# A fixed order for the Strassen products of a 256-token stage, with the next unit's first product ahead of the odd unit's seventh

## The chip, the cores and the metric

One Trainium2 chip, one of its cores. The metric is the device time of one execution in microseconds (us), lower is better; a kernel's figure is the median of several runs. Each core has five engines that work side by side and wait for one another through semaphores: TensorE (matrix products; PE in the profile, PEld for its weight loads), VectorE (DVE), ScalarE (ACT), GpSimd (POOL) and SyncE (SP). Each engine runs its own instructions strictly in the order in which the program lists them.

## The reference

Attention over 8 batches of 12 heads (448 tokens, head size 64), and its output, reshaped to 3584 tokens of 768 values, through a gated feed-forward block:

```python
def _attn_ref(q, k, v):
    scale = 1.0 / np.sqrt(q.shape[-1])
    scores = scale * np.matmul(q, k.transpose(0, 1, 3, 2))
    scores = scores - np.max(scores, axis=-1, keepdims=True)
    attn = np.exp(scores)
    attn = attn / (np.sum(attn, axis=-1, keepdims=True) + 1e-09)
    return np.matmul(attn, v).astype(np.float32)

def _moe_ref(x, w_gate, w_val, w_out):
    g = x @ w_gate                          # 3584x768 by 768x1536
    silu = g * (1.0 / (1.0 + np.exp(-g)))
    val = x @ w_val
    return (silu * val @ w_out).astype(np.float32)
```

## The kernel before

The kernel works in float16 with float32 sums. Attention goes over pairs of heads; the feed-forward block for tokens that are ready is woven between attention steps, so that TensorE always has something to do. When attention is over, two stages are left in which the first half of the feed-forward block (gate and value products) is computed with Strassen's method in its seven-product form: one of 256 tokens by 256 tokens (the subject here), and one later of 448 by 448. Between them and at the end come groups of output products (`out_group`, L694).

**A unit.** The class `Unit` covers two of the 12 blocks of 128 feature rows, for gate (even unit number u) or value (odd u), and two halves of tokens. There are 12 units, 0 to 11. The 768 input values are split in two halves, so each unit is a 2x2 by 2x2 block product, and its four result blocks need seven products P1 to P7 instead of eight. A product (L817) is three matmuls of 128x128 weights by 128x256 tokens, into one of three PSUM areas: `a` and `e`, the two banks of a tile `un` (three such tiles in rotation), and `b`, a tile `ub` (two in rotation). The steps of one unit, and what each waits for:

- P1 starts `a`. A1 (ScalarE, L859) copies `a` to `b`. P2 then adds to `a`, whose sum is result block 00.
- P5 starts `e`. A2 (ScalarE, L863) copies `e` to SBUF, into a buffer `kept` (p5).
- P6 adds to `b`, after A1. D1 (VectorE, L866) writes `b` + p5 into `e`, after P6 and A2. P3 then adds to `e`: result block 01.
- P7 adds to `b`, after D1, which has to read `b` first. D2 (VectorE, L870) writes `b` + p5 into a second `kept` buffer in SBUF: result block 11.
- P4 adds to `b`, after D2, which has to read `b` first: result block 10.
- F00, F01, F10 and F11 read the four result blocks out. Of a gate unit ScalarE does it (L882: silu into SBUF); of a value unit VectorE does it (L884: silu times value, to `hts`). The two value blocks in `un` and the one in `ub` are in PSUM; block 11 lies in SBUF as `kept`, so F11 of an odd unit reads both of its inputs, silu and `kept`, from SBUF.

So five of the seven products wait for nothing but P1's or P5's place or for copies made early, while P6 waits for A1, P7 for D1 and P4 for D2: between these, products of the neighbouring unit are put in.

**What sets the order.** `unit_items` makes a dictionary of items: name (such as `P6_4`, product P6 of unit 4), engine, a duration taken for it, the names that it comes after, and the function that emits it. `order_of` plans the items of all engines with these durations, and with a latency from engine to engine (0.22 us behind TensorE, 0.07 behind VectorE and ScalarE): again and again it takes the item that could start first, or one on the same engine within 0.12 us of it that stands earlier in the dictionary. The instructions are emitted in the order of the planned starts, and each engine then runs its own in that order. Nothing is planned anew on the chip.

**Beside the units.** GpSimd makes the sums of weights that P3, P5, P6 and P7 take as stationary operand (`weight_sums`, L780 to L783: four sums of 128x384 elements of float16, items `W_6` to `W_11`), well ahead of the units that need them, and after them half of the sums for the first output group (L555 to L558, items `G0` to `G7`). All of these read and write SBUF. Item `O` is one output product group (L665) that stands ahead of the last P4.

Of the kernel before, what the change touches and what calls it, by code (L numbers as in the profile page):

```python
# [65 lines left out]
def kernel(  # L66
# [17 lines left out]
    NFB = DF // 128  # L84
# [358 lines left out]
    def pv_open(pr, one=False):  # L443
        if one:
            acc = ps_s.tile([128, 2, 512], FP32, tag="s", name="acc")
            accs[pr] = [acc[:, hx] for hx in range(2)]
        else:
            accs[pr] = [ps_f.tile([128, 512], FP32, tag="f", name="acc") for _ in range(2)]
# [457 lines left out]
    with tc.manual_schedule():  # L906
# [424 lines left out]
        def unit_items(units, make, w):  # L1331

            items = {}
            t_pe, t_act, t_dve = NK * (w / 2400 + 0.0025), 0.2 + w / 1280, 0.2 + w / 1050

            def begin(u):
                units[u] = make(u)
                units[u].P1()

            for u in range(NFB):  # L1340
                old_s = [f"{k}_{u - 3}" for k in ("F00", "F01")] if u > 2 else []
                old_f = [f"{k}_{u - 2}" for k in ("F10", "D2")] if u > 1 else []
                items[f"P1_{u}"] = (PE_, t_pe, old_s, lambda u=u: begin(u))

                def do(name, eng, us, after, u=u):
                    items[f"{name}_{u}"] = (eng, us, after, lambda: getattr(units[u], name)())

                if u < 2:
                    do("Z", PE_, t_pe / NK, old_f)
                    old_f = [f"Z_{u}"]  # L1350
                do("A1", ACT_, t_act, [f"P1_{u}"] + old_f)
                do("P5", PE_, t_pe, [f"P1_{u}", f"W_{u}"])
                do("A2", ACT_, t_act, [f"P5_{u}"] + ([f"D2_{u - 2}"] if u > 1 else []))
                do("P6", PE_, t_pe, [f"A1_{u}"])
                do("D1", DVE_, t_dve, [f"P6_{u}", f"A2_{u}"])
                do("P7", PE_, t_pe, [f"D1_{u}"])
                do("D2", DVE_, t_dve, [f"P7_{u}"] + ([f"F11_{u - 2}"] if u > 1 else []))
                do("P3", PE_, t_pe, [f"D1_{u}"])
                do("P4", PE_, t_pe, [f"D2_{u}"])
                do("P2", PE_, t_pe, [f"A1_{u}"])  # L1360
                for f, bb, last in ((0, 0, "P2"), (1, 1, "D2"), (1, 0, "P4"), (0, 1, "P3")):
                    name = f"F{f}{bb}"
                    items[f"{name}_{u}"] = (
                        DVE_ if u % 2 else ACT_,
                        t_dve if u % 2 else t_act,
                        [f"{last}_{u}"] + ([f"{name}_{u - 1}"] if u else []),
                        lambda u=u, f=f, bb=bb: units[u].out(f, bb),
                    )
            return items
# [5 lines left out]

        units = {}
        items = unit_items(units, lambda u: Unit(u, 256, x5, t5, hts5), 256)
        p0 = NPAIR - 1
        pv_open(p0, True)
        pv_rest(p0)  # L1380
# [38 lines left out]
        items = unit_items(units, lambda u: Unit(u, S, x7, t7, hts), S)  # L1419
# [14 lines left out]
        for m, fn in enumerate(final[0][0][1]):  # L1434
            u = NFB - 1 if m else NH - 1
# [35 lines left out]
```

## Time and profile before

| | us |
|---|---|
| time before, median of 3 runs | 428.84 |
| lowest and highest of them | 428.45, 429.25 |
| the profiled execution's own time | 429.01 |
| its span (first to last instruction) | 427.2 |
| TensorE busy in it | 419.4 |
| the stage of 256 tokens, first product to first output group | 299.90 to 329.31 |
| in 299.9 to 329.3: VectorE, ScalarE, GpSimd busy | 21.04, 16.81, 28.93 |

The times of single instructions are from the profiled execution, counted from its span's start. A row of the timeline has the start in us, the duration in us, engine, line of the kernel, operation, what is written and read (`ub<-vraw,wg` writes the tile `ub` and reads `vraw` and `wg`; names are those of the buffer's first use, so sums of weights and tokens appear as `E`, `vraw`, `qkraw`, `wsum` or `vo`), sizes, the count of instructions merged into the row, and in brackets the engine's idle time before the row and what ended it. A product's row of three matmuls has a duration of 0.49 us, while the next product can start 0.33 us after it: matmuls overlap, so stalls of TensorE are seen in the distance of starts, not in the gaps. VectorE's and ScalarE's rows overlap a little for the same reason. The granted TensorE clock is 1.00 throughout this stage.

### The profile page before, as it was taken

To read this page: it belongs to the slowest core of one execution; us is meant where nothing else is said; L and a number is where in the kernel's file an instruction comes from. 1 tells how busy PE (TensorE), PEld (TensorE's weight loads), DVE (VectorE), ACT (ScalarE), POOL (GpSimd) and SP (SyncE) were. 2 spreads that over 40 slices of the span, in tenths; PEclk is the share of its full clock that TensorE was granted. 3 is DMA by queue.
4 is the path that set the end of the run, shared out by engine and by line. 5 is a ranking of instruction groups with operands and counts; after the bars stand their busy time and mean duration, and the time that the engine had idled before them with its cause. 6 is when DMAs were issued, how large, how long until landed. Compare 5 with 4: busy or idle time off the path is not lost.

```text
span 427.2 us, 11656 instructions
## 1 busy us (share of the span) xinstructions
PE 419.4 (98%) x4652; PEld 290.4 (68%) x4652; DVE 269.7 (63%) x644; ACT 245.1 (57%) x395; POOL 229.8 (54%) x351
## 2 busy tenths in 40 slices
PE   8999999999999999999999999999999999999996
PEld 3666666655457777757666677777889985555795
DVE  4766562776568665575635776677777765565663
ACT  6975667646656655646666546559655235545221
POOL 8656525989885683657654774945999000000000
PEclk9999999999999999999999999999999999999999
DMA  9999999999999699999999997923100241000125
GB/s 138 177 200 200 200 177 187 140 153 213 173 136 127 97 193 106 163 122 114 123 153 127 141 155 91 153 47 97 23 1 21 94 107 44 0 2 1 38 76 149
DMA packets 107927, 49.77 MB, mean 116 GB/s; under 512 B 59872, under 2 KB 104672, under 8 KB 107872
## 3 DMA queue, kind: packets, MB, share of 16 engines
q0 software_dynamic: 46800, 24.56, 51.5%
q1 hardware_dynamic: 60752, 24.22, 32.4%
q8 instruction: 36, 0.59, 0.6%
q10 hardware_dynamic: 320, 0.25, 0.2%
q14 instruction: 19, 0.16, 0.1%
HBM read 49.55 MB, written 11.01 MB: 142 GB/s over the span
## 4 chain that ended last, share of the span: by engine, by line
PE 92%; ACT 3%; DVE 3%; issue 1%; DMA 0%; ACTq 0%; DVEq 0%
PE gp L572 17%; PE og L694 17%; PE vp L572 12%; PE un L817 10%; PE acc L435 8%; PE ub L817 8%; PE s L344 5%; PE op L665 5%; PE acc L400 2%; PE s L374 2%; PE s L356 1%; ACT E L382 1%; PE tp L317 1%; PE op L1023 1%; PE wp L164 1%; DVE t L625 1%
## 5 line engine op out<-in xcount | busy, mean ns | idle before, releaser
L364 ACT ACTIVATE E<-s 128x896 f16<-128x896 f32 x126 | 106.6, 918 | 40.2 <-PE s L344 28.2
L572 PE MATMUL gp<-X,wg 128*128 128x384 f16 (+1 forms) x360 | 73.9, 347 | 0.0
L238 POOL COPY qk<-qkraw 128x512 f16<-128x512 f16 x70 | 42.9, 655 | 55.1 <-DMA qkT<-qk 54.6
L572 PE MATMUL vp<-X,wv 128*128 128x384 f16 (+3 forms) x360 | 66.7, 321 | 0.1
L625 DVE SCALAR_TENSOR_TENSOR t<-sg,gp 128x384 f32<-128x384 f32 (+1 forms) x60 | 36.3, 607 | 42.3 <-ACT sg L599 42.0
L572 PEld LDWEIGHTS <-wv 128*128 128x128 f16 x462 | 43.7, 98 | 25.8 <-issue 0.3
L572 PEld LDWEIGHTS <-wg 128*128 128x128 f16 x360 | 32.8, 98 | 26.3 <-issue 2.1
L178 POOL DMA_DIRECT2D vraw<-in_v_dram x72 | 44.0, 634 | 12.2 <-DMA wo<-in_moe_w_out_dram 8.2
L599 ACT ACTIVATE sg<-gp 128x384 f32<-128x384 f32 (+1 forms) x60 | 32.1, 537 | 28.6 <-PE gp L572 27.9
L382 ACT ACTIVATE E<-s 112x896 f16<-112x896 f32 x48 | 40.6, 917 | 8.7 <-PE s L374 8.7
L178 POOL DMA_DIRECT2D qkraw<-in_k_dram x70 | 42.4, 622 | 5.0 <-DMA wo<-in_moe_w_out_dram 3.6
L435 PEld LDWEIGHTS <-E 128*128 128x128 f16 (+1 forms) x1152 | 37.5, 96 | 10.8 <-issue 4.7
L694 PEld LDWEIGHTS <-hts 128*128 128x128 f16 x528 | 44.1, 98 | 0.3
L435 PE MATMUL acc<-vo,E 128*128 128x65 f16 (+1 forms) x1152 | 42.2, 192 | 0.8 <-DVE hts L631 0.6
L631 DVE SCALAR_TENSOR_TENSOR hts<-t,vp 128x384 f16<-128x384 f32 (+3 forms) x60 | 32.5, 541 | 5.9 <-PE vp L572 1.9
L465 DVE TENSOR_TENSOR xt<-acc,R 128x256 f16<-128x256 f32 x72 | 30.6, 425 | 2.5
L719 ACT ACTIVATE osb<-og 128x384 f32<-128x384 f32 x21 | 10.3, 491 | 38.0 <-PE og L694 38.0
L201 POOL DMA_DIRECT2D qkraw<-in_q_dram x43 | 29.3, 682 | 5.0 <-DMA vraw<-in_v_dram 2.2
L344 PE MATMUL s<-qkT 64*128 64x448 f16 x216 | 30.2, 354 | 0.2
L694 PE MATMUL og<-wo,hts 128*128 128x192 f16 x264 | 29.0, 246 | 0.0
L694 PEld LDWEIGHTS <-hsum 128*128 128x128 f16 x300 | 25.5, 98 | 1.0
L464 DVE RECIPROCAL R<-acc 128x4 f32<-128x4 f32 x72 | 12.7, 177 | 18.0 <-PE acc L435 17.9
(184 smaller groups left out, 713.2 us busy)
## 6 DMA issues: line engine op xcount, KB each, us to landing
vraw<-in_v_dram POOLq DMA_DIRECT2D x72, 64.0 KB, 4.7
qkraw<-in_q_dram POOLq DMA_DIRECT2D x39, 112.0 KB, 4.5
qkraw<-in_k_dram POOLq DMA_DIRECT2D x68, 64.0 KB, 4.5
wg<-in_moe_w_gate_dram POOLq DMA_DIRECT2D x8, 288.0 KB, 10.1
wv<-in_moe_w_val_dram POOLq DMA_DIRECT2D x8, 288.0 KB, 10.6
wo<-in_moe_w_out_dram POOLq DMA_DIRECT2D x2, 1152.0 KB, 18.3
out_dram<-osb SPq DMA_DIRECT2D x7, 288.0 KB, 3.7
out_dram<-osb SPq DMA_DIRECT2D x6, 336.0 KB, 3.2
```

Source lines behind the costliest of these rows:

```text
L178: eng.dma_start(dst[ts(s, 64)], rows)
L238: nc.gpsimd.tensor_copy(dst.rearrange("p c h d -> p h c d"), src)
L344: nc.tensor.matmul(s[:, hx, 0:S], lhsT=t[ts(hx, 64), ts(c + low(pr, hx), 128)], rhs=t[ts(hx, 64), ds(NC * 128, S)], start=True, stop=True,)
L364: nc.scalar.activation(e[:, 0 : 2 * S].rearrange("p (h q) -> p h q", h=2), s[:, :, 0:S], AF.Exp, scale=sm_scale)
L382: nc.scalar.activation(e[:, :, 0:S], s[0:P, :, 0:S], AF.Exp, scale=sm_scale)
L435: nc.tensor.matmul(acc[:, ts(j, D + 1)], lhsT=e[rows, ds(hx * S + j * 128, 128)], rhs=Vts[pr % NV][rows, hx, col, 0 : D + 1], start=first, ...
L572: nc.tensor.matmul(dst[:, 0:w], lhsT=wslice(kind, self.fb, cb), rhs=X[kk][:, cb, ds(c0 + lo, w)], start=(cb == 0), stop=(cb == NCB - 1),)
L599: self.readers = [nc.scalar.activation(self.sg[:, 0:n], gp[:, 0:n], AF.Tanh, scale=0.5)]
L625: nc.vector.scalar_tensor_tensor(self.t1[:, 0:n], self.sg[:, 0:n], 1.0, self.gp[:, 0:n], ALU.add, ALU.mult)
L631: nc.vector.scalar_tensor_tensor(self.hts[:, self.fb, ds(lo, w)], self.t1[:, ds(lo, w)], 0.5 * HS, vp[:, 0:w], ALU.mult, ALU.mult)
L694: nc.tensor.matmul(dst, lhsT=lhs(n), rhs=rhs(n), start=first and n == 0, stop=n == NH - 1, skip_group_check=True)
L817: mm = nc.tensor.matmul(dst, lhsT=lhs[:, n], rhs=rhs[:, n], start=first and n == 0, stop=n == NK - 1, skip_group_check=True,)
```

## The change

Behind the making of the items, a list of product names is written out, and each name in it is made to wait for the one ahead of it. The planner and everything behind it stay as they are, and so do the stage of 448 tokens and units 0 and 1 up to their last products.

```diff
         units = {}
         items = unit_items(units, lambda u: Unit(u, 256, x5, t5, hts5), 256)
+        names = ["P1_2", "P5_2"]
+        for u in range(2, NFB, 2):
+            names += f"P6_{u} P4_{u - 1} P2_{u} P1_{u + 1} P5_{u + 1} P7_{u} P3_{u} P6_{u + 1} P4_{u}".split()
+            names += f"P2_{u + 1} P1_{u + 2} P7_{u + 1} P3_{u + 1} P5_{u + 2}".split()
+        names = [name for name in names if name in items]
+        for one, two in zip(names, names[1:]):
+            items[two][2].append(one)
```

`NFB` is 12. The line of names makes, for each even u from 2 to 10, one chain over the products of units u and u+1, beginning with P6 of u and ending with P5 of u+2; names of units that don't exist are dropped, so behind P3 of unit 11 the chain ends.

## The prediction

> **What bounds the kernel now.** I read the page from the top: the busy shares, then the chain that ended last.
>
> ```profile
> span 427.2 us, 11656 instructions
> PE 419.4 (98%) x4652; PEld 290.4 (68%) x4652; DVE 269.7 (63%) x644; ACT 245.1 (57%) x395; POOL 229.8 (54%) x351
> ...
> PE 92%; ACT 3%; DVE 3%; issue 1%; DMA 0%; ACTq 0%; DVEq 0%
> ```
>
> TensorE is busy for 98% of the span and holds 92% of the chain. Only TensorE's own stalls can be removed, and every new stall of TensorE moves the end. The changed stage runs from 299.90 us (the first product of unit 0) to 329.31 us (the first output group), 29.4 us long. I then read TensorE's timeline there; one row is one product of three matmuls. The first four rows are the first and fifth product of unit 2, the fourth of unit 1 and the sixth of unit 2; the last three are the fourth product of unit 2 and the second and seventh of unit 3.
>
> ```profile
> 304.47 0.49 PE L817 MATMUL un<-X,wg 128*128 128x256 f16 x3
> 304.80 0.49 PE L817 MATMUL un<-vraw,qkraw 128*128 128x256 f16 x3
> 305.13 0.49 PE L817 MATMUL ub<-vraw,wv 128*128 128x256 f16 x3
> 305.48 0.49 PE L817 MATMUL ub<-vraw,qkraw 128*128 128x256 f16 x3
> ...
> 307.79 0.49 PE L817 MATMUL ub<-vraw,wg 128*128 128x256 f16 x3
> 308.12 0.49 PE L817 MATMUL un<-X,wv 128*128 128x256 f16 x3
> 308.52 0.49 PE L817 MATMUL ub<-vraw,wsum 128*128 128x256 f16 x3
> ```
>
> Starts lie 0.327 us apart when nothing waits (304.47 to 304.80; 14 products without a stall would take 4.58 us). The pair of units from 307.79 to 312.50 takes 4.70 us, so it stalls for 0.12 us. The rows show where: the seventh product of an odd unit starts 0.40 after the second instead of 0.327 (net 0.078 each time), and the two steps between products of the two `ub` banks take 0.35 (net 0.022 each). The profile shows no other idle time of TensorE here, so this is **all that any order can win**: over the stage's five pairs after the first, about 0.6 us, or 0.14% of the run.
>
> **The order that results.** By the planner's rule and its listed durations, TensorE's order before is P1 P5 P4' P6 P2 (even unit u, prime for u-1), then P1 P5 (u+1), P7 P3 (u), P6 (u+1), P4 (u), P2 P7 P3 (u+1). The change makes two edits per pair from unit 2 on. P6 of u goes ahead of P4 of u-1. P1 of u+2 goes ahead of P7 of u+1, so four times: units 4, 6, 8, 10. VectorE keeps its order (F10 of u-1, then D1 of u), except that D1 of unit 2 goes ahead of F10 of unit 1. ScalarE and GpSimd keep theirs. No instruction is added or removed, and no DMA moves.
>
> **Edit one, P1 of u+2 ahead of P7 of u+1.** P7 of an odd unit waits for D1, which ends 0.05 us before it. With one product more between P6 and P7 there are four, 4 x 0.327 = 1.31 us; the chain from P6 through D1 took 308.52 - 307.44 = 1.08. So these four stalls go: 4 x 0.078 = 0.31 saved. P6 of u+2 now stands four products behind its P1 instead of three, so the wait for copy A1 goes too, for units 4 to 10: 4 x 0.022 = 0.09 saved. The early P1 needs the `un` bank of u-1, whose last reader ended 3.2 us earlier (306.02 against 309.18 for unit 4): nothing lost. The stall before P4 of u is untouched (P7, P3, P6, P4 still in a row). Unit 11 has no successor, so the stall of its P7 stays. Saved together: 0.40.
>
> **Edit two, P6 of u ahead of P4 of u-1.** P6 waits for copy A1 of its unit.
>
> ```profile
> 305.06 0.37 ACT L859 ACTIVATE ub<-un 128x256 f32<-128x256 f32 x1 [1.03 <-PE un L817]
> ```
>
> For unit 2, P1 isn't moved (nothing stands ahead of it in the list). A1 ends at 305.43 and P6 can start at 305.48 at the earliest, exactly where it is. P4 of unit 1 filled that time and now comes after it: **0.33 lost**, once. For units 4 to 10 the moved P1 gives the cover back.
>
> **What is late next: VectorE.** P7 of an odd unit is now one product nearer to P7 of the next even one: eight products (2.62 us) instead of nine. Between them lies a chain on VectorE.
>
> ```profile
> 309.05 0.42 DVE L870 TENSOR_TENSOR kept<-ub,kept 128x256 f32<-128x256 f32 x1
> 309.58 0.77 DVE L884 SCALAR_TENSOR_TENSOR hts<-silu,kept 128x256 f16<-128x256 f32 x1
> 310.27 0.41 DVE L884 SCALAR_TENSOR_TENSOR hts<-silu,un 128x256 f16<-128x256 f32 x1
> 310.60 0.41 DVE L884 SCALAR_TENSOR_TENSOR hts<-silu,ub 128x256 f16<-128x256 f32 x1
> 310.93 0.42 DVE L866 TENSOR_TENSOR un<-ub,kept 128x256 f32<-128x256 f32 x1
> ```
>
> These are D2, F11, F01, F10 of unit 3 and D1 of unit 4, without a gap between the last four. D2 starts 0.53 after P7 starts (308.52), F11 0.53 after D2; from the end of F11 to P7 of unit 4 it is -0.08 (the next starts that much before the end) + 0.33 + 0.33 + 0.42 + 0.05 (VectorE's end to TensorE's start, as at 308.52) = 1.05. (F10 also waits for P4 of u-1, which edit two makes a product later; it would let F10 of unit 3 start at 310.94, earlier than the chain does below, so it holds up neither F10 nor the D1 queued behind it.) So P7 of u can start no sooner than P7 of u-1 + 1.06 + F11 + 1.05. With F11 at 0.43 that is 2.54, inside the 2.62. With the 0.77 of this row it is 2.88: a stall. Before, nine products (2.95 and 0.02) covered it, with 0.14 to spare for unit 4. So **F11 decides**, and it is the one whose time varies.
>
> ```profile
> L884 DVE SCALAR_TENSOR_TENSOR hts<-silu,kept x6: 426/680/814, 304.9 to 328.4; 128x256 f16<-128x256 f32 x6
> L884 DVE SCALAR_TENSOR_TENSOR hts<-silu,kept x6: 625/626/626, 358.2 to 397.9; 128x448 f16<-128x448 f32 x6
> ```
>
> Its six in this stage take 426 to 814 ns; the same line with 448 tokens, later, when the page shows POOL at 0, always 625 or 626. GpSimd's rows give the reason:
>
> ```profile
> 309.15 0.91 POOL L781 TENSOR_TENSOR E<-E,wg 128x384 f16<-128x384 f16 x1
> 310.02 1.09 POOL L782 TENSOR_TENSOR E<-wg,wg 128x384 f16<-128x384 f16 x1
> 311.08 0.91 POOL L783 TENSOR_TENSOR E<-wg,E 128x384 f16<-128x384 f16 x1
> ```
>
> F11 of unit 3 ends at 310.34, 0.28 after the GpSimd sum that ran when it came (310.06), and the next sum takes 1.09 instead of 0.91. The same holds for all six: the end is 0.28 after a sum's end. F11 (both inputs in SBUF) and a sum hold each other up. The Trainium skill, SBUF — State Buffer, section "Who interferes with whom", says that a VectorE instruction with two SBUF inputs and a GpSimd instruction that reads SBUF exclude each other for a whole instruction, the first one winning; the trace agrees, with these 0.28 and 1.09. Were the port shared evenly instead, each F11 would take the 0.66 that is the mean of the six, and units 4 to 10 would each stall for 1.06 + 0.66 + 1.05 - 2.62 = 0.15: +0.53 in all, in four small stalls and not in one large.
>
> **The sum.** P6 of unit 2 at 305.48, then eleven products and one 0.02: P7 of unit 3 at 309.10 (before 308.52), F11 at 310.16. The sum of L781 ends at 310.06 as before, and L782 has run since 310.02, undisturbed now: it ends at 310.93. F11 ends at 311.21 and P7 of unit 4 starts at 312.26; its turn was 309.10 + 2.62 = 311.72. **Stall 0.55.** From there six products and 0.02 to P7 of unit 5 (314.25), F11 at 315.31, GpSimd's L783 (from 314.67, 0.91) ends at 315.58, F11 at 315.86, P7 of unit 6 at 316.91 where its turn was 316.87: 0.04. The same reckoning gives 0.04 for units 8 and 10, because GpSimd's sums come round every 4.65 us, like a pair. P7 of unit 11: 327.95 instead of 327.34. In parts: +0.33 +0.55 +0.12 -0.40 = **+0.60**. The row bounds of F11's hold are 0 (it slips in at 310.06) and 0.72 (a whole sum of 0.87 plus the 0.28, less 0.43); I take 0.63, because it comes 0.14 after the start of L782, and all six rows waited for the sum that had begun. Behind the stage TensorE's output groups follow without gaps (329.31, 329.81, 330.30), so 0.60 reaches the end. The profiled execution took 429.01 (span 427.2 and 1.8 around it): 429.6 against that, and **429.4** against the median of 428.84, which lies 0.17 below it.
>
> **Rivals.**
> *F11 of unit 3 slips in* (0.2): it comes 0.10 after the sum's end at 310.06; should the hand-over be later or the phase of the sums differ by that much, F11 takes 0.43, unit 4's turn is missed by 0.02 only, and so on. +0.33 - 0.40 + 4 x 0.03 = +0.05: 428.9. Against it: the next sum is listed as started at 310.02.
> *A second miss, the slower side* (0.1): F11 of unit 5 comes at 315.31, 0.26 ahead of a sum's end. If GpSimd runs that much earlier against TensorE, it meets the following sum, and P7 of unit 6 pays some 0.55 more: +1.15, 430.0. It decides from a shift of 0.25. For it: both chains feed back on each other. Against: the lock holds them in step once they have met.
> *The order pays as written* (0.07): VectorE never holds P7, and A1 of unit 2 comes early enough: -0.40, 428.4. Against it: A1 ends 0.05 before P6 in the rows.
> The remaining 0.05 is for waits that no row shows. That the order isn't taken up can't be: each name is made to wait for the one ahead.
>
> **The numbers.** The forecast has 0.58: 429.4, itself between 429.1 and 429.8. The range 428.6 to 430.1 takes in the slip-in and most of the second miss. A measurement of this kernel tells some 0.2%, 0.86 us, from no change. Faster by that (below 427.98) is out of reach of the 0.6 that the stage stalls for: 0.03. Slower (above 429.70): the second miss and the upper edge of the forecast, 0.22. Same: 0.75.
>
> **What will show it.** P6 of unit 2 should start 0.68 after P5 of unit 2, and its P4 of unit 1 behind it. P7 of units 3, 5, 7, 9 should start 0.327 after the product before. F11 of unit 3 should take about 1.05, and P7 of unit 4 start 0.88 after P5 of unit 5; those of units 6, 8, 10 some 0.37. The forecast is wrong if F11 of unit 3 takes under 0.6, or if TensorE stalls beyond unit 4 by over 0.1.

## The result and the profile after

The changed kernel takes 430.0 us (median of 12 runs, 429.26 to 431.52) against 428.79 us for the kernel before in the same comparison. The ratio is 1.0031 with a 95% interval of 1.0024 to 1.0039: slower by 1.2 us by the medians, twice the forecast 0.60, and with the whole interval above the 0.2% that the forecast lay within. The page of the profiled execution (430.36 us), its span, its busy shares and the chain that ended last:

```profile
span 428.6 us, 11651 instructions
...
PE 419.6 (98%) x4652; PEld 290.2 (68%) x4652; DVE 270.1 (63%) x644; ACT 245.4 (57%) x395; POOL 229.5 (54%) x351
...
PE 90%; DVE 4%; ACT 3%; DMA 1%; issue 1%; ACTq 0%; DVEq 0%; SPq 0%
```

TensorE does the same work; its share of the chain falls from 92 to 90% and VectorE's rises from 3 to 4%. From the first product of unit 0 to the start of the last P4 the stage took 29.09 us before (299.90 to 328.98) and takes 30.45 now (299.88 to 330.32): 1.36 more, and the span is 1.4 longer. The piece of the chain behind it, 252 matmuls of the output groups, takes 20.79 us in both, so the whole difference arises in this stage and reaches the end.

TensorE's timeline shows where. Rows as in the prediction; the brackets at the end, which no row of before had in this stage, give TensorE's idle time and what ended it. In order: P5 and P6 of unit 2, P4 of unit 1; P5 of unit 5 and P7 of unit 4; P5 of unit 11 and P7 of unit 10.

```profile
304.78 0.49 PE L817 MATMUL un<-vraw,qkraw 128*128 128x256 f16 x3
305.46 0.49 PE L817 MATMUL ub<-vraw,qkraw 128*128 128x256 f16 x3 [0.19 <-ACT ub L859]
305.78 0.49 PE L817 MATMUL ub<-vraw,wv 128*128 128x256 f16 x3
...
311.37 0.49 PE L817 MATMUL un<-vraw 128*128 128x256 f16 x3
312.25 0.49 PE L817 MATMUL ub<-vraw,E 128*128 128x256 f16 x3 [0.38 <-DVE un L866]
...
325.94 0.49 PE L817 MATMUL un<-vraw,vo 128*128 128x256 f16 x3
326.94 0.49 PE L817 MATMUL ub<-vraw,wsum 128*128 128x256 f16 x3 [0.52 <-DVE un L866]
```

A step beyond 0.327 is a stall. The table lists those that differ, in us beyond 0.327, from the starts of the products:

| stall before | kernel before | forecast | changed kernel |
|---|---|---|---|
| P6 of unit 2 | 0.02 | 0.35 | 0.35 |
| P6 of units 4, 6, 8, 10 | 0.02 each | 0 | 0 |
| P7 of units 3, 5, 7, 9 | 0.08 each | 0 | 0 |
| P7 of unit 4 | 0 | 0.55 | 0.55 |
| P7 of units 6 and 8 | 0 | 0.04 each | 0.11 each |
| P7 of unit 10 | 0 | 0.04 | 0.68 |

Everything up to P7 of unit 4 came as worked out. The rest is 0.11 instead of 0.04 at units 6 and 8, and a second hold of F11 at unit 10. VectorE's rows for F11 of units 3 and 9:

```profile
310.13 1.05 DVE L884 SCALAR_TENSOR_TENSOR hts<-silu,kept 128x256 f16<-128x256 f32 x1
...
324.70 1.19 DVE L884 SCALAR_TENSOR_TENSOR hts<-silu,kept 128x256 f16<-128x256 f32 x1
```

and GpSimd's around the first, then two sums of the pair between (taken up further below), and those around the second, where a row with x2 holds two sums, each but a held one 0.91 long:

```profile
310.00 0.91 POOL L782 TENSOR_TENSOR E<-wg,wg 128x384 f16<-128x384 f16 x1
310.87 1.09 POOL L783 TENSOR_TENSOR E<-wg,E 128x384 f16<-128x384 f16 x1
...
319.30 0.91 POOL L780 TENSOR_TENSOR vo<-wv 128x384 f16<-128x384 f16 x1
320.29 0.97 POOL L781 TENSOR_TENSOR vo<-vo,wv 128x384 f16<-128x384 f16 x1
...
322.96 1.78 POOL L555 TENSOR_TENSOR hsum<-hts 128x384 f16<-128x384 f16 x2
324.70 1.96 POOL L556 TENSOR_TENSOR hts<-hts 128x384 f16<-128x384 f16 x2
```

F11 of unit 3 comes at 310.13, after the sum of L782 has begun, waits for that whole sum (to 310.91) and ends 0.28 later. F11 of unit 9 comes at 324.70, 0.04 ahead of the end of the sum that runs then (324.74); that is too late, the next sum, the first of L556, goes first (to 325.61), and F11 ends 0.28 after it.

### The profile page after: what moved, and what is told of

Read it like the earlier page. It is cut to its first block, busy times and chain, and to the rows that moved or that the text cites. A ratio compares the mean times of both kernels' runs of the same rounds, so it can differ in the third digit from the quotient of the medians.

```text
span 428.6 us, 11651 instructions
## 1 busy us (share of the span) xinstructions
PE 419.6 (98%) x4652; PEld 290.2 (68%) x4652; DVE 270.1 (63%) x644; ACT 245.4 (57%) x395; POOL 229.5 (54%) x351
## 4 chain that ended last, share of the span: by engine, by line
PE 90%; DVE 4%; ACT 3%; DMA 1%; issue 1%; ACTq 0%; DVEq 0%; SPq 0%
PE gp L572 17%; PE og L694 17%; PE vp L572 12%; PE un L817 9%; PE acc L435 8%; PE ub L817 8%; PE s L344 5%; PE op L665 5%; PE acc L400 2%; PE s L374 2%; PE s L356 1%; ACT E L382 1%; PE tp L317 1%; PE op L1023 1%; DVE t L625 1%; DVE hts L631 1%
```

## Experiments

The theory after the result: edit one saves 0.40; edit two costs 0.33 at unit 2; and with eight products between the seventh ones a hold of F11 by a whole GpSimd sum reaches TensorE, twice in this execution (0.55 and 0.68), beside 0.11 at units 6 and 8, where F10 waits for P4 and D1 stands behind it. Rivals: that the order itself makes the loss (the shorter distance, whatever F11 takes), or that only one of the edits does.

The effects are near what timing can tell, so each run is read in two ways: its ratio to the kernel before in the same comparison (whose median was 428.64 to 428.79), and the length of the stage in its profiled execution, from the first product of unit 0 to the start of the last P4, which shows single stalls but is one execution.

| run | median us | ratio to before, 95% interval | stage, us | against 29.09 |
|---|---|---|---|---|
| changed kernel | 430.0 | 1.0031 (1.0024 to 1.0039) | 30.45 | +1.36 |
| changed kernel, once more | 429.95 | one run | 30.44 | +1.35 |
| edit one alone | 428.71 | 0.9999 (0.9989 to 1.0009) | 28.83 | -0.26 |
| edit two alone | 430.35 | 1.0040 (1.0028 to 1.0053) | 30.73 | +1.64 |
| F11 from PSUM | 429.1 | 1.0020 (1.0009 to 1.0032) | 29.43 | +0.35 |
| GpSimd later | 429.02 | 1.0006 (0.9991 to 1.0021) | 29.43 | +0.35 |
| before, F11 from PSUM | 429.07 | 1.0002 (0.9990 to 1.0014) | 29.21 | +0.12 |
| D1 ahead of F10 | 428.81 | 0.9999 (0.9988 to 1.0010) | 29.43 | +0.34 |
| P4 of unit 1 first | 428.88 | 0.9993 (0.9975 to 1.0012) | 29.10 | +0.02 |
| all mends | 428.43 | 0.9987 (0.9975 to 0.9999) | 28.51 | -0.58 |

**Edit one alone.**

```diff
-            names += f"P6_{u} P4_{u - 1} P2_{u} P1_{u + 1} P5_{u + 1} P7_{u} P3_{u} P6_{u + 1} P4_{u}".split()
+            names += f"P4_{u - 1} P6_{u} P2_{u} P1_{u + 1} P5_{u + 1} P7_{u} P3_{u} P6_{u + 1} P4_{u}".split()
```

> Only edit one: the next unit's P1 ahead of the odd unit's P7, with P4 left ahead of P6. Theory (the head stall of unit 2, and F11 held by a GpSimd sum in the shortened VectorE chain, make the loss): no stall at P6 of unit 2; F11 of unit 3 comes at 309.83 and meets the sum that ends near 310.06, so it ends at 310.34 as before the change, and P7 of unit 4 has its turn at 311.42; every later F11 gets in 0.3 to 0.6 us before a sum's end in the same way. P7 of unit 11 at 327.1, 0.25 us ahead of before: about 428.5. Rival (the shorter distance between the seventh products costs by itself): P7 of units 4 to 10 late as in the changed kernel, at least 0.5 us slower than before.

The stage is 0.26 shorter, the 0.25 of the theory, with no stall above 0.03 between P7 of unit 1 and P7 of unit 11. (The 0.02 at P6 of units 4 to 10 is gone, but P4 of the odd unit, now three products behind P7 and not four, waits for D2 by as much.) F11 of units 3 to 9 takes 0.50 to 0.55. The distance between seventh products is the eight of the changed kernel, so that distance alone costs nothing: the rival falls. In the times the gain can't be told from zero (interval 0.9989 to 1.0009).

**Edit two alone.**

```diff
-            names += f"P2_{u + 1} P1_{u + 2} P7_{u + 1} P3_{u + 1} P5_{u + 2}".split()
+            names += f"P2_{u + 1} P7_{u + 1} P3_{u + 1} P1_{u + 2} P5_{u + 2}".split()
```

> Only edit two: P6 ahead of P4, with P1 left behind P7 and P3. Theory: A1 is too late for P6 in each of units 2, 4, 6, 8 and 10, so each P6 starts 0.68 us after P5 instead of 0.33 and nothing fills it: 5 x 0.33 = 1.65 us, 430.4. The distance from P7 of an odd unit to P7 of the next is nine products and that stall, so F11 costs nothing. Rival (edit one makes the loss, edit two is worth little): within 0.4 us of before.

TensorE's timeline has such a row for each of the five pairs (the fifth bracket names GpSimd, but there too A1 ends 0.05 ahead, at 325.61 against 325.66); the first two:

```profile
305.53 0.49 PE L817 MATMUL ub<-vraw,qkraw 128*128 128x256 f16 x3 [0.19 <-ACT ub L859]
310.56 0.49 PE L817 MATMUL ub<-vraw,E 128*128 128x256 f16 x3 [0.19 <-ACT ub L859]
```

Five steps of 0.68 instead of 0.35, the stage 1.64 longer, 430.35 us. Edit two needs edit one, in every pair. F11 of units 5 and 9 was held to 0.90 and 0.89 here and cost nothing: with nine products and a stall of A1 between the seventh ones there is room for it.

**F11 from PSUM.** Once F00 has read bank `a` out, D2 of an odd unit can put block 11 there instead of into SBUF; F11 then has one input in each memory.

```diff
     def D2(self):
+        if self.u % 2 and self.w == 256:
+            self.c22 = self.a
+            self.note(DVE_, nc.vector.tensor_tensor(self.a, self.b, self.p5, ALU.add), "a")
+            return
...
```

Two more lines, left out here, make D2 of an odd unit wait for F00 and enter F11 among the readers of that bank.

> The changed kernel, with block 11 of the odd units written to the PSUM bank a that F00 has read out, so that F11 has one input in SBUF and one in PSUM. Theory: F11 takes about 0.42 us in all six units, whatever GpSimd runs, and the sums take 0.91; the stalls of 0.55 and 0.68 at P7 of units 4 and 10 fall to the 0.11 that units 6 and 8 show (F10 waits for P4, and D1 behind it). +0.33 - 0.40 + 4 x 0.11 = +0.35 against before: 429.1. Rival (the order stalls P7 through VectorE's queue whatever F11 takes): the time of the changed kernel, 430.0.

VectorE's group of all readouts of `un` (F00, F01 and now F11, 18 in all; minimum, median and maximum in ns):

```profile
L889 DVE SCALAR_TENSOR_TENSOR hts<-silu,un x18: 414/422/422, 303.5 to 329.1; 128x256 f16<-128x256 f32 x18
```

None is held, though GpSimd runs as before, and its sums take 0.91 beside them. The stalls at P7 of units 4, 6, 8 and 10 are 0.11 each: of the 0.55 and 0.68 the holds made 0.44 and 0.57, and F10's wait of 0.11 is left. The stage is 0.35 longer than before, as worked out. In the times alone this isn't clear: the interval overlaps that of the changed kernel, and 0.35 us (a ratio of 1.0008) lies just below it.

**GpSimd later.** One more instruction on GpSimd, on an idle tile, ahead of the weight sums of unit 6.

```diff
+        items["N"] = (POOL_, 0.4, [], lambda: nc.gpsimd.tensor_add(warm[:], warm[:], warm[:]))
+        items["W_6"][2].append("N")
```

> The changed kernel with one more GpSimd instruction (128x128, a sum of an unused tile with itself) ahead of the weight sums of unit 6: GpSimd's later sums all come some 0.3 to 0.4 us later, nothing else is touched. Theory (only the phase of the sums decides): F11 of unit 3 now comes ahead of the end of the sum of L781 and gets in behind it, 0.28 us after its end, so P7 of unit 4 stalls by about 0.1 and not 0.55; the added work makes the kernel 0.4 us faster or more if unit 9 gets in too: 429.1 to 429.6. Rival (the sums only fill GpSimd's time): no change from 430.0.

The added instruction took 0.40 us. Ahead of P7 of unit 4, VectorE's F11 of unit 3 and GpSimd's sums around it:

```profile
309.83 0.54 DVE L884 SCALAR_TENSOR_TENSOR hts<-silu,kept 128x256 f16<-128x256 f32 x1
```

```profile
309.17 0.91 POOL L781 TENSOR_TENSOR E<-E,wg 128x384 f16<-128x384 f16 x1
310.05 1.09 POOL L782 TENSOR_TENSOR E<-wg,wg 128x384 f16<-128x384 f16 x1
```

Counted from the stage's first product (299.57 here, 299.88 in the changed kernel), F11 comes at 10.26 against 10.25, and L781's sum begins at 9.60 against 9.25. So F11 now comes 0.25 ahead of the end of L781's sum (310.08) instead of 0.09 behind it, gets in there and takes 0.54, not 1.05; it is L782's sum that gives way (1.09). All four stalls are 0.11, also that of unit 10. **More work made the kernel faster**, by 1.0 us of stage and from a ratio of 1.0031 to 1.0006. The phase of GpSimd's sums (how they lie in time against TensorE's products) decides over both holds: the order is the changed kernel's, and both are gone.

**The control: the kernel before with F11 from PSUM** (the same edit on the order before).

> The control: the kernel before with block 11 of the odd units in the PSUM bank a, as in the run that did this to the changed kernel. Theory (F11 costs only where eight products stand between the seventh ones, not nine): F11 falls to 0.42 in all six units as well, and nothing else moves, 0.0 us, the stage from the first product to the last P4 29.09 us as before. Rival (F11 in PSUM is faster in itself, whatever the order): some 0.5 to 1 us faster than before.

F11 fell to 0.42 here too and no stall went: the long F11 of before was covered. The stage is 0.12 longer, all of it one new stall at P7 of unit 10, where D1 waited for a product of `un`, 0.28 us after VectorE was free. Why only there isn't settled; the ratio is 1.0002.

**D1 ahead of F10.**

```diff
+        for u in range(2, NFB, 2):
+            items[f"F10_{u - 1}"][2].append(f"D1_{u}")
```

> The changed kernel with D1 of the even unit put ahead of F10 of the odd one on VectorE, units 4 to 10. Theory: F11 of unit 3 is still held to 0.28 us after the sum of L782 (1.05 us), but one instruction of 0.33 less stands between it and D1, so P7 of unit 4 stalls by 0.21 and not 0.55; the 0.11 of units 6 and 8 falls to 0.05 or less, and VectorE comes early enough for F11 of unit 9 to get in. +0.33 - 0.40 + 0.21 + 0.1 = +0.24: 428.9. Rival (VectorE's queue isn't what P7 waits for): the changed kernel's 430.0.

F11 of unit 3 was held to 1.05 again and P7 of unit 4 stalled by 0.22 (0.21 expected); the 0.11 of units 6 and 8 went, and F11 of unit 9 took 0.66. So P7 does wait for VectorE's queue, and the 0.11 is F10's wait in it. The total missed, +0.34 and not +0.24: F10 comes later now, and copy A1 of unit u+1, which writes the bank that F10 reads, waits for it. ScalarE's row for A1 of unit 5:

```profile
311.76 0.37 ACT L859 ACTIVATE ub<-un 128x256 f32<-128x256 f32 x1 [0.65 <-DVE hts L884]
```

P6 of units 5, 7 and 9 stalled by 0.13, 0.06 and 0.07 for it. A wait taken out of one engine's queue came back by way of another.

**P4 of unit 1 first.**

```diff
+        names[2:4] = names[3:1:-1]
```

> The changed kernel with P4 of unit 1 ahead of P6 of unit 2, the one pair that has no P1 ahead of it; later pairs as in the change. Theory: the 0.33 at P6 of unit 2 goes, everything behind it comes 0.33 earlier, and that alone lets F11 of unit 3 come at 309.8, ahead of the end of the sum at 310.1: P7 of units 4, 6, 8, 10 stalls by 0.11 each. -0.40 + 4 x 0.11 = +0.04: 428.7; F11 of unit 9 comes within 0.1 us of a sum's end, and if it misses that, 429.3. Rival (only the 0.33 goes, the stall at P7 of unit 4 is the order's): 429.7.

The 0.33 at P6 of unit 2 is gone, and with it both holds: F11 of unit 3 takes 0.51, of unit 9 0.42, and the four stalls are 0.10 to 0.11. One product put back, worth 0.33, takes 1.34 from the stage, since everything behind it comes at another phase of the sums.

**The changed kernel once more.**

> The changed kernel once more, for its trace. Theory: F11 of unit 3 comes 0.09 to 0.10 us after the end of a sum and is held in every execution (1.05 us, P7 of unit 4 late by 0.55); F11 of unit 9 comes within 0.05 us of a sum's end, so it may be held (P7 of unit 10 late by 0.68, span 428.6) or get in (late by 0.11, span 428.0). Rival (the second hold is as fixed as the first): 0.68 again.

F11 of unit 9 came 0.02 to 0.03 ahead of a sum's end, again too late, and P7 of unit 10 stalled by 0.68 again (unit 4: 0.54). Both traces of the changed kernel have both holds, as the rival has it; two traces don't show that F11 of unit 9 is held in every execution.

**All mends together.**

```diff
-        names = ["P1_2", "P5_2"]
+        names = ["P1_2", "P7_1", "P3_1", "P5_2"]
         for u in range(2, NFB, 2):
-            names += f"P6_{u} P4_{u - 1} P2_{u} P1_{u + 1} P5_{u + 1} P7_{u} P3_{u} P6_{u + 1} P4_{u}".split()
-            names += f"P2_{u + 1} P1_{u + 2} P7_{u + 1} P3_{u + 1} P5_{u + 2}".split()
+            names += f"P6_{u} P4_{u - 1} P2_{u} P1_{u + 1} P5_{u + 1} P7_{u} P3_{u} P6_{u + 1} P2_{u + 1}".split()
+            names += f"P4_{u} P1_{u + 2} P7_{u + 1} P3_{u + 1} P5_{u + 2}".split()
...
+            items[f"F10_{u - 1}"][2].append(f"D1_{u}")
```

with block 11 in PSUM as above.

> All the mends together: the list begins with P1 of unit 2 ahead of P7 of unit 1, P2 of the odd unit stands ahead of P4 of the even one, D1 ahead of F10 on VectorE, and block 11 of odd units in PSUM. Theory: every stall of the stage but the one before P7 of unit 11 (0.08) goes; the kernel before has 0.75 us of them: 0.65 us faster than before, 428.0, and the stage takes 28.4 us against 29.09. Rival (the stalls come back elsewhere, in ScalarE's or VectorE's queue): within 0.2 us of before.

Of the stage's stalls two are left, 0.02 before P4 of unit 0 and 0.10 before P7 of unit 11. The stage takes 28.51 us, 0.58 less than before. The time is 428.43 us, the lowest median here, with a ratio of 0.9987 (0.9975 to 0.9999): faster than the kernel before by a margin that the interval only just clears. The expected 0.65 counted each stall whole; the step behind a stall is 0.325, not 0.327, and unit 11's is longer.

## Why the prediction was right and wrong

**The bound** was right: TensorE's stalls in the stage are all that the order can move, and 1.36 us of them are the 1.4 of the span.

**Edit one** was right: the four stalls of 0.08 and the four of 0.02 went in every run that had it; with edit one alone the four of 0.02 came back at P4 of the odd unit.

**Edit two** was right: 0.35 at P6 of unit 2, and 0.33 in each pair where P1 isn't moved (edit two alone). One thing in the description of the unit has to be put right for this: P6, P7 and P4 wait for A1, D1 and D2, so four of the seven products are free to fill in, not five.

**What is late next** was right in kind and, for unit 4, in size: F11 behind the sum of L782, 1.05 us, P7 of unit 4 at 312.25 against the 312.26 worked out. F11 from PSUM and the later GpSimd show that this is the cause. The lock as the Trainium skill has it (SBUF — State Buffer, "Who interferes with whom") agrees with the traces: F11, which comes at 310.13 after L782's sum has begun, waits for all of it, and with one input in PSUM F11 isn't touched (0.41 to 0.42). The even sharing that was set against it, four stalls of 0.15, isn't what happened. One term was a little too wide: the 0.14 to spare before the change ran from D1's end and still held the 0.05 to TensorE's start; by the prediction's own sum (2.97 less 2.88) it was 0.09.

**The step that failed** is this one: "The same reckoning gives 0.04 for units 8 and 10, because GpSimd's sums come round every 4.65 us, like a pair." The stall of unit 10 was 0.68, and those of units 6, 8 and 10 together 0.90 and not 0.12; stalls of over 0.1 beyond unit 4 are the prediction's own second sign of being wrong. Two terms behind the step were mis-sized, and each had a row in the trace of before.

- The stall of units 6 and 8 was 0.11, not 0.04. F10 was taken to follow P4 by 0.04. Here it follows P4's end by 0.11 (the end of P4 of unit 5 is 316.03, F10 starts at 316.13), as D1 follows P6 of an odd unit; before, F10 of unit 9 had this 0.11 too (324.43 to 324.54). Twice 0.065 brings F11 of unit 9 later by 0.13.
- The sum behind F11 was taken to end 0.18 late in each pair. Behind F11 of unit 7 it is L781's, which starts after a pause of 0.08 that GpSimd makes there anyway: it took 0.97, not 1.09, and began no later than without F11. The row of 305.48 before the change had shown 0.97 for the same place. So GpSimd came 0.12 earlier than a period of 4.65 would have it.

The rows of P4 and F10 of unit 5 in the changed kernel, for the first of the two:

```profile
315.54 0.49 PE L817 MATMUL ub<-vraw,wv 128*128 128x256 f16 x3
```

```profile
316.13 0.42 DVE L884 SCALAR_TENSOR_TENSOR hts<-silu,ub 128x256 f16<-128x256 f32 x1
```

Together they used up nearly all of the 0.26 by which F11 of unit 9 was to come ahead of a sum's end: it came 0.04 ahead, which was too late. The rival of a second miss had the mechanism, a deciding shift of 0.25 and its time (430.0), but put it at unit 6 and gave it 0.1, since the lock was to hold both chains in step; that its time came out to the tenth is in part luck, with another unit and another sum of stalls. The chains stay in step only while their periods agree: a pair with a stall of 0.11 takes 4.71 us, and GpSimd's five sums took 4.53 (320.21 to 324.74) with F11 in their pause.

**The rest**: the rival that F11 of unit 3 slips in didn't occur in either trace, and took place when the head stall was taken away or GpSimd delayed. Nothing behind the stage gave anything back.

## What to carry to other kernels

When a new order shortens the distance between two steps on the bounding engine, add up the longest of the chain on the other engines between them, with the largest duration in the trace and not the median, since a cover that hid an occasional long instruction goes along with the stall. Here a duration that varied for one shape was a wait for a lock: find what such an instruction ends with, and then carry the phase of both sides forward pair by pair, with the row of the same place and not with a mean period. Taking the operand out of the contended memory removed the hold in every F11 of the three kernels that did it (18 of them); delaying GpSimd, or putting one product back, removed it by a shift in phase only, so such a cure rests on the phase that it happens to make.

## What the runs showed of the hardware

A VectorE instruction that came 0.02 to 0.04 us ahead of the end of a GpSimd sum lost to the next one (unit 9 twice; F11 of unit 1 in the run with GpSimd later, 304.55 against 304.57, took 1.17), while ones that came 0.09 ahead (323.96 against 324.05 in that run, 0.43 long; 323.69 against 323.78 with P4 of unit 1 first, 0.42) and more got in. So in these traces the hand-over lies between 0.04 and 0.09 us before the end that the profile lists, and 0.05 us of phase are worth some 0.6 us here (a stall of 0.68 against 0.11).
